# Moving the start addresses of the activation rooms of a routed expert layer: h to 96 and x to 192 modulo 256 bytes

## The chip, the cores and the metric

The kernel runs on one core of one Trainium2 chip. The metric is the device time of one execution in microseconds (us). Lower is better.

## What is computed

The reference is an attention over pooled keys and values, followed by a layer in which each token goes to one of eight experts, if a linear score lets it be computed at all:

```python
# attention: batch 8, 8 heads, 576 positions, head size 64; keys and values pooled by 8 (72 of them)
k_p = k.reshape(B, H, Sp, pool, D).mean(axis=3)
v_p = v.reshape(B, H, Sp, pool, D).mean(axis=3)
scores = scale * np.matmul(q, k_p.transpose(0, 1, 3, 2))
attn = softmax(scores)
x = np.matmul(attn, v_p)              # 4608 tokens of 512
# experts: w1 is 8 x 512 x 1024, w2 is 8 x 1024 x 512
do_compute = x @ w_skip > 0
e_idx = np.argmax(x @ w_gate, axis=1)
h = np.maximum(x[mask] @ w1[e], 0.0)
out = x + gate_w * (h @ w2[e])        # tokens with do_compute; the others keep x
```

## The kernel before

All data are float32. The kernel has two stages.

**Attention** runs over 36 tiles of 128 tokens. Per tile TensorE computes scores (L321), transposes the exponentials (L346, L350) and multiplies with the pooled values (L364, L366), in plain float32. Results are stored to the output by SyncE's queue (`out<-x`), and a routing step sorts the tokens to their experts.

**The experts** run in units of up to three tiles (384 tokens) of one expert. A product in this stage is made of three TensorE products of numbers split in a high and a low part (float32r): high x high, high x low and low x high. The order of work is fixed: a loop over units on each engine, coupled by semaphores. In one unit TensorE does this:

- the **first layer** (`first`, L1136 to L1138): for each of 8 slices f of h and each of 4 slices k of x, three matmuls. The stationary operand is a 128x128 piece of `w1hi` or `w1lo`, the moving operand a slice of `xhi` or `xlo` of as many columns as the unit has tokens, 256, 288, 320 or 384. These are 96 matmuls in a row.
- the **second layer** (`second`, L1151, L1152, L1154): for each tile of 128 tokens and each of 8 slices k of h, two or three matmuls. The stationary operand is a 128x128 piece of `hhi` or `hlo`, the moving operand 512 columns of `w2hi` or `w2lo`.

ScalarE writes `hhi` from the first layer's result (L1192), VectorE writes `hlo` (L1249). ScalarE and VectorE also make `xhi` and `xlo` of the next unit (L1201, L1270) and split the next expert's weights (L1183, L1216). GpSimd gathers tokens into `ring` (L1049) and scatters results (L1054). The first piece of the expert work (L515 to L517, L530 to L532, two tiles of the first expert) is woven into the end of the attention stage and uses the same four rooms and the same weights.

**Where tiles lie.** Tiles of the pool `cp` lie one behind the other along a partition. Four of them are the rooms that the change moves: `xhi`, `xlo` (6144 bytes each in the expert stage) and `hlo`, `hhi` (12288 bytes each). While the attention runs, the same rooms hold inputs: `xhi` and `xlo` are two of the three buffers of q, `hlo` and `hhi` the two buffers of v. The function `early` (L144) makes a room for its first use, and puts an unused tile of `gaps[name]` bytes ahead of it; `late` (L139) makes the room for the experts at the same place. The rooms stand in the order xhi, hlo, xlo, hhi; behind them stand the tiles of the attention's pools.

With the numbers of before, `xhi` and `xlo` begin at 160 modulo 256 bytes, `hlo` and `hhi` at 128. The weights `w1hi`, `w2hi`, `w1lo`, `w2lo` stand ahead of all this and begin at 128 modulo 256. Slices of these tiles are whole multiples of 256 bytes apart (x: 1536 per k, w1: 4096 per k and 512 per f, h: 1536 per k and 512 per tile, w2: 2048 per k), so each operand of the experts' matmuls begins where its tile begins, modulo 256.

Of the kernel before, what the change touches and what calls it, by code (L numbers as in the profile page):

```python
# [110 lines left out]
def emit(tc, q, k, vm, vr, wg, w1, w2, cf, out):  # L111
    nc = tc.nc
    with ExitStack() as top:
        cp = top.enter_context(tc.tile_pool(name="const", bufs=1))
        dp = top.enter_context(tc.tile_pool(name="dram", bufs=1, space=DRAM))
        whi = cp.tile([128, 4, F], F32R, name="w1hi"), cp.tile([128, 8, D], F32R, name="w2hi")
        wlo = cp.tile([128, 4, F], F32R, name="w1lo"), cp.tile([128, 8, D], F32R, name="w2lo")
        table = dp.tile([NE * NTOK + 128, RT], F32, name="table")
        cfs = cp.tile([128, cf.shape[1]], F32, name="cfs")
        wgs = cp.tile([128, 108], F32, name="wgs")  # L120
        c = dict(ident=cfs[:, 0:128], epos=cfs[:, 384:392], first=cfs[:, 392:400], unit=cfs[:, 436:437], place=cfs[:, 443:444], third=cfs[:, 444:445], wgs=wgs,
                 pair=cfs[:, 445 + UNITS:453 + UNITS].rearrange("p (g h) -> p g h", h=2), next=cfs[:, 445:445 + UNITS], left=cfs[0:4 * KL, 439:443])
        c["lower"] = cp.tile([128, 128], BF16, name="upper")
        c["ones"] = cp.tile([128, 128], BF16, name="ones")
        pay = cp.tile([128, NT, RT], F32, name="pay")
        offs = cp.tile([128, NE], F32, name="offs")
        slot = cp.tile([128, SLOTS], I32, name="slot")
        gate = cp.tile([128, SLOTS], F32, name="gate")
        nti = cp.tile([128, 2 * UNITS + 1], I32, name="nti")
        near = dict(ids=cp.tile([128, 2, 2], F32, name="nids"), slot=cp.tile([128, 2], I32, name="nslot"),  # L130
                    first=cp.tile([128, NE], F32, name="nfirst"), jt=cp.tile([128, NE], F32, name="njt"),
                    place=cp.tile([128, 1], F32, name="nplace"))

        stage = cp.tile([128, NST, F], F32, name="stage")
        b = dict(stage=stage)

        gaps = dict(xhi=160, hlo=224, xlo=32, hhi=224)

        def late(name):  # L139

            s, dt = {"x": ([128, 4, 384], F32R), "h": ([128, 8, 384], F32R), "r": ([128, 6, RW], F32)}[name[0]]
            b[name] = cp.tile(s, dt, name=name)

        def early(name, *s):  # L144
            if gaps.get(name):
                cp.tile([128, gaps[name] // 4], F32, name=f"gap{name}")
                gaps[name] = 0
            return cp.tile(list(s), F32, name=name)

        def load_constants():  # L150
            nc.sync.dma_start(cfs[:, 128:], cf[:, 128:])
            nc.sync.dma_start(wgs, wg)

        def spread_constants():
            nc.gpsimd.memset(near["jt"], float(JT))
            nc.gpsimd.memset(nti, 0)
            nc.gpsimd.tensor_copy(c["lower"], cfs[:, 128:256])
            nc.gpsimd.tensor_copy(c["ones"], cfs[:, 256:384])
            nc.gpsimd.memset(pay, 0.0)
            nc.gpsimd.tensor_copy(pay[:, :, 0], cfs[:, 400:436])  # L160
            nc.gpsimd.tensor_copy(offs, c["first"])
            nc.gpsimd.tensor_copy(near["first"], c["first"])

        with tc.manual_schedule(engines={mybir.EngineType.PE, mybir.EngineType.Activation, mybir.EngineType.DVE, mybir.EngineType.Pool}):
            held = attention(tc, nc, q, k, vm, vr, cf, w1, w2, whi, wlo, out, c, pay, offs, table, load_constants, spread_constants, near, b, late, early,
                      dict(slot=slot, gate=gate, nti=nti))
        with tc.tile_pool(name="moeps", bufs=1, space=PSUM) as pp:
            experts(tc, nc, out, w1, w2, whi, wlo, slot, gate, nti, held, near, b, c["ident"], pp)
# [1170 lines left out]
```

## Time and profile before

| | |
|---|---|
| median of 3 runs | 544.38 us (543.05 to 544.89) |
| the profiled execution | 544.18 us |
| its span, from first to last instruction | 542.4 us |
| TensorE (PE) busy | 509.2 us, 94% of the span |
| VectorE, ScalarE, GpSimd busy | 54%, 45%, 40% |
| mean granted TensorE clock | 0.975 |

A busy TensorE in this profile is one that has some matmul in flight: matmuls overlap, so the duration of one is longer than the distance to the next. How fast a stream of matmuls runs is read from the start times in the timeline. The 1.8 us between the time and the span lie ahead of the first and behind the last instruction.

### The profile page before, as it was taken

How to read it: one execution, taken by the hardware profiler on the slowest of the kernel's cores; microseconds unless marked ns; L12 is line 12 of the kernel's file. 1: busy time of each engine (PE TensorE's matmuls, PEld its weight loads, DVE VectorE, ACT ScalarE, POOL GpSimd, SP SyncE). 2: the span in 40 equal slices, each digit the busy share in tenths (PEclk: the TensorE clock that was granted, in tenths of full speed). 3: DMA queues.
4: the chain of work that ended last, by engine and by line, in shares of the span. 5: the costliest groups of instructions: out<-in, count | busy, mean ns of one | idle time of the engine just before them, and what ended most of it. 6: DMA issues, size and time to landing. Idle time of an engine off the chain costs nothing. (4 is left out here: it accounts for less than half of the span.)

```text
span 542.4 us, 10998 instructions
## 1 busy us (share of the span) xinstructions
PE 509.2 (94%) x3350; PEld 460.7 (85%) x3351; DVE 295.2 (54%) x698; ACT 244.2 (45%) x671; POOL 215.6 (40%) x294
## 2 busy tenths in 40 slices
PE   6899999999799888999999999999999999999994
PEld 3789899888688677888989899998989898989893
DVE  4476878877477621344624553232355656665563
ACT  5488889898551011141514142211334435544441
POOL 4725565899966333112321232332321132314042
PEclk8699999999799999999999999999999999999998
DMA  8999979975662111116421551111145647463200
GB/s 293 364 344 338 350 253 368 311 231 195 220 202 70 30 36 51 41 47 209 153 74 39 187 182 63 39 63 51 57 174 162 213 148 271 161 213 104 95 30 7
DMA packets 35799, 87.30 MB, mean 161 GB/s; under 512 B 7529, under 2 KB 9961, under 8 KB 33968
## 3 DMA queue, kind: packets, MB, share of 16 engines
q1 hardware_dynamic: 27648, 72.80, 38.8%
q0 software_dynamic: 8112, 14.03, 8.0%
q8 instruction: 18, 0.29, 0.2%
q14 instruction: 21, 0.17, 0.1%
HBM read 74.04 MB, written 21.52 MB: 176 GB/s over the span
## 5 line engine op out<-in xcount | busy, mean ns | idle before, releaser
L1136 PE MATMUL psl<-xhi,w1hi 128*128 128x256 f32 (+3 forms) x416 | 122.2, 294 | 4.2 <-PEq L965 3.2
L1137 PE MATMUL psl<-xlo,w1hi 128*128 128x256 f32 (+3 forms) x416 | 121.5, 292 | 0.0
L1138 PE MATMUL psl<-xhi,w1lo 128*128 128x256 f32 (+3 forms) x416 | 121.5, 292 | 0.0
L1192 ACT ACTIVATE hhi<-psl 128x256 fp32r<-128x256 f32 (+4 forms) x104 | 41.9, 403 | 152.7 <-ACTq L965 151.7
L1054 POOL DMA_INDIRECT out<-ring,slot x39 | 39.5, 1012 | 176.4 <-POOLq L965 158.9
L1151 PE MATMUL psf<-w2hi,hhi 128*128 128x512 f32 x240 | 94.9, 395 | 2.8 <-PEq L965 2.8
L1152 PE MATMUL psf<-w2lo,hhi 128*128 128x512 f32 x240 | 93.7, 390 | 0.0
L1249 DVE SCALAR_TENSOR_TENSOR hlo<-psl,hhi 128x256 fp32r<-128x256 f32 (+2 forms) x104 | 43.8, 423 | 79.8 <-DVEq L965 79.3
L1136 PEld LDWEIGHTS psl<-xhi,w1hi 128*128 128x128 f32 x416 | 78.3, 188 | 6.1 <-issue 5.5
L1137 PEld LDWEIGHTS psl<-xlo,w1hi 128*128 128x128 f32 x416 | 78.3, 188 | 0.4
L1138 PEld LDWEIGHTS psl<-xhi,w1lo 128*128 128x128 f32 x416 | 78.3, 188 | 0.0
L1154 PE MATMUL psf<-w2hi,hlo 128*128 128x512 f32 x200 | 78.1, 391 | 0.0
L335 ACT ACTIVATE e<-sc,nm 128x72 f32<-128x72 f32 x288 | 64.6, 342 | 0.5 <-DVE nm L328 0.3
L1238 DVE SCALAR_TENSOR_TENSOR ring<-psf,ring 128x512 f32 x25 | 18.7, 750 | 75.5 <-DVEq L965 75.5
L1151 PEld LDWEIGHTS psf<-w2hi,hhi 128*128 128x128 f32 x240 | 45.1, 188 | 11.8 <-issue 3.2
L1152 PEld LDWEIGHTS psf<-w2lo,hhi 128*128 128x128 f32 x240 | 45.1, 188 | 8.6
L1049 POOL DMA_INDIRECT ring<-out,slot x39 | 43.8, 1123 | 16.1 <-issue 12.9
L364 PE MATMUL o<-blocks,pT 128*128 128x148 f32 (+1 forms) x304 | 49.1, 298 | 1.0 <-DVE x L388 0.6
L1201 ACT ACTIVATE xhi<-psd 128x512 fp32r<-128x512 f32 x36 | 18.9, 599 | 68.4 <-ACTq L965 68.4
L328 DVE TENSOR_REDUCE nm<-sc 128x4 f32<-128x288 f32 x72 | 32.4, 453 | 24.8 <-PE sc L321 22.7
L1154 PEld LDWEIGHTS psf<-w2hi,hlo 128*128 128x128 f32 x200 | 37.6, 188 | 8.0
L364 PEld LDWEIGHTS o<-blocks,pT 128*128 128x128 f32 (+1 forms) x304 | 40.9, 183 | 2.9 <-issue 0.8
(220 smaller groups left out, 871.2 us busy)
## 6 DMA issues: line engine op xcount, KB each, us to landing
stage<-in_w SPq DMA_DIRECT2D x64, 512.0 KB, 4.4
out<-x SPq DMA_DIRECT2D x36, 256.0 KB, 4.9
stage<-in_k SPq DMA_DIRECT2D x6, 1152.0 KB, 9.4
hlo<-in_vm SPq DMA_DIRECT2D x4, 1024.0 KB, 8.2
hhi<-in_vm SPq DMA_DIRECT2D x4, 1024.0 KB, 8.6
xlo<-in_q SPq DMA_DIRECT2D x6, 512.0 KB, 5.6
qt<-in_q SPq DMA_DIRECT2D x6, 512.0 KB, 6.8
xhi<-in_q SPq DMA_DIRECT2D x5, 512.0 KB, 7.0
```

The costliest lines, as they stand in the source:

```text
L335: nc.scalar.activation(e[:, h, :], sc[h // 4][:, h % 4 * SP:(h % 4 + 1) * SP], AF.Exp, bias=nm[:, h:h + 1], scale=-1.0)
L364: nc.tensor.matmul(o_[sl, g * 2 * VA:(g + 1) * 2 * VA], pT[:, 2 * a + g, sl], vbd[b % 3][:, 2 * a + g, :], start=(g == 0), stop=False)
L1049: g.indirect_dma_start(ring[:, s % 6, 0:D], None, out, bass.IndirectOffsetOnAxis(ap=slot[:, s:s + 1], axis=0), bounds_check=NTOK - 1, oob_ ...
L1054: g.indirect_dma_start(out, bass.IndirectOffsetOnAxis(ap=offsets, axis=0), ring[:, s % 6, 0:D], None, bounds_check=NTOK - 1, oob_is_err=Fa ...
L1136: t.matmul(ps, whi[0][:, k, w], xhi[:, k, xs], start=(k == 0), stop=False)
L1137: t.matmul(ps, whi[0][:, k, w], xlo[:, k, xs], start=False, stop=False)
L1138: last = t.matmul(ps, wlo[0][:, k, w], xhi[:, k, xs], start=False, stop=(k == 3))
L1151: t.matmul(ps, hhi[:, k, sl], whi[1][:, k, :], start=(k == 0), stop=False)
L1152: last = t.matmul(ps, hhi[:, k, sl], wlo[1][:, k, :], start=False, stop=(short and k == 7))
L1154: last = t.matmul(ps, hlo[:, k, sl], whi[1][:, k, :], start=False, stop=(k == 7))
L1192: a.activation(hhi[:, f, xs], psL[f % 3][:, xs], AF.Relu).then_inc(sem["act"], 1)
L1249: m = v.scalar_tensor_tensor(to[:, f], psL[f % 3][:, cs], 0.0, hhi[:, f, cs].bitcast(F32), ALU.max, ALU.subtract)
```

## The change

Four numbers change, the bytes of the unused tiles ahead of the four rooms. No instruction is added, removed or moved: on every engine the program has the same instructions in the same order, with other addresses.

```diff
-        gaps = dict(xhi=160, hlo=224, xlo=32, hhi=224)
+        gaps = dict(xhi=192, hlo=160, xlo=96, hhi=160)
```

What follows for the starts of tiles, modulo 256 bytes:

| tiles | before | after |
|---|---|---|
| w1hi, w1lo, w2hi, w2lo | 128 | 128 |
| stage, ring | 160 | 160 |
| xhi, xlo | 160 | 192 |
| hlo, hhi | 128 | 96 |
| qt and kp (third buffer of q, pooled keys) | 128 | 96 |
| vl, vs, e, pT, p4, x (the attention's) | 0 | 224 |
| blocks (pooled keys and values as moving operands) | 192 | 160 |

All tiles behind `hhi` move by 32 bytes, since the four gaps sum to 608 bytes in place of 640.

## Rows read from the trace of the kernel before

**Rows 1.** Busy time by stage: the whole program in three stretches (attention, the passage with the first expert work, the units of experts). Columns: the stretch in us, its length, busy us (and instructions) of each engine, granted TensorE clock, share of the DMA engines, GB/s.

```profile
0.00:182.00 182.00, 165.41 (x1255) 149.60 (x1257) 128.95 (x415) 127.89 (x472) 117.54 (x172) 0.94 0.75 264
182.00:220.00 38.00, 32.19 (x191) 27.52 (x190) 11.24 (x24) 6.34 (x14) 11.41 (x15) 0.96 0.15 42
220.00:542.40 322.40, 311.60 (x1908) 283.59 (x1906) 155.01 (x261) 109.95 (x185) 86.61 (x108) 0.99 0.35 117
```

**Rows 2.** What TensorE waited for between 220 and 500 us: us in total, times, longest.

```profile
PE psf L1151 <- PEq L965: 1.1, 1, 1.1
PE psl L1136 <- issue: 0.9, 1, 0.9
PE psl L1136 <- PEq L965: 0.9, 2, 0.5
```

**Rows 3.** Timeline of TensorE, first and last rows of one first-layer pass with 256 columns: start in us, duration, instruction. From the first row to the last there are 96 matmuls.

```profile
356.71 0.28 PE L1136 MATMUL psl<-xhi,w1hi 128*128 128x256 f32 x1
356.83 0.28 PE L1137 MATMUL psl<-xlo,w1hi 128*128 128x256 f32 x1
...
367.80 0.28 PE L1138 MATMUL psl<-xhi,w1lo 128*128 128x256 f32 x1
367.91 0.39 PE L1151 MATMUL psf<-w2hi,hhi 128*128 128x512 f32 x1
```

**Rows 4.** The same of a second pass with 256 columns, and the busy times of the two passes (columns as in the first group).

```profile
437.36 0.28 PE L1136 MATMUL psl<-xhi,w1hi 128*128 128x256 f32 x1
...
448.56 0.39 PE L1151 MATMUL psf<-w2hi,hhi 128*128 128x512 f32 x1
...
356.71:367.91 11.20, 11.20 (x97) 11.20 (x96) 3.72 (x8) 2.70 (x7) 3.49 (x5) 1.00 0.20 67
437.38:448.58 11.20, 11.20 (x98) 11.20 (x97) 7.04 (x11) 6.29 (x11) 3.54 (x5) 1.00 0.44 144
```

**Rows 5.** Timeline, passes with 288 columns (first row, and the first row behind its 96 matmuls), with 320 columns (second matmul and last of the 96, so 94 distances) and with 384 columns (first row, and the first row behind its 96 matmuls).

```profile
460.80 0.30 PE L1136 MATMUL psl<-xhi,w1hi 128*128 128x288 f32 x1
...
473.61 0.39 PE L1151 MATMUL psf<-w2hi,hhi 128*128 128x512 f32 x1
...
225.48 0.31 PE L1137 MATMUL psl<-xlo,w1hi 128*128 128x320 f32 x1
...
239.27 0.31 PE L1138 MATMUL psl<-xhi,w1lo 128*128 128x320 f32 x1
...
403.17 0.34 PE L1136 MATMUL psl<-xhi,w1hi 128*128 128x384 f32 x1
...
420.13 0.39 PE L1151 MATMUL psf<-w2hi,hhi 128*128 128x512 f32 x1
```

**Rows 6.** Timeline of the second layer, first and last of 18 matmuls in a row with 512 columns (17 distances).

```profile
329.62 0.39 PE L1151 MATMUL psf<-w2hi,hhi 128*128 128x512 f32 x1
329.85 0.39 PE L1152 MATMUL psf<-w2lo,hhi 128*128 128x512 f32 x1
...
333.47 0.39 PE L1154 MATMUL psf<-w2hi,hlo 128*128 128x512 f32 x1
```

**Rows 7.** Timeline of the same kind of matmul where the granted clock is 0.5 (five distances from the first row to the last).

```profile
187.79 0.63 PE L530 MATMUL sc<-w2hi,hhi 128*128 128x512 f32 x1
...
189.92 0.63 PE L532 MATMUL sc<-w2hi,hlo 128*128 128x512 f32 x1
```

**Rows 8.** Timeline of the attention's plain float32 matmuls with pooled values (a row joins four matmuls of 148 columns, or two), with the granted clock at 1.

```profile
121.01 0.67 PE L364 MATMUL o<-blocks,pT 128*128 128x148 f32 x4
121.51 0.42 PE L366 MATMUL o<-vl,p 128*128 128x148 f32 x2
121.77 0.41 PE L321 MATMUL sc<-blocks,qt 128*128 128x144 f32 x2
```

**Rows 9.** Groups by line and shape: how many matmuls of each shape there are (L1137 and L1138 have as many as L1136), the weight loads, and the two engines that follow the first layer. Columns: count, busy us, mean ns, idle before.

```profile
L1136 PE MATMUL psl<-xhi,w1hi 128*128 128x256 f32 x256 | 72.0, 281 | 3.3 <-PEq L965 3.2
L1136 PE MATMUL psl<-xhi,w1hi 128*128 128x320 f32 x96 | 29.9, 311 | 0.9 <-issue 0.9
L1136 PE MATMUL psl<-xhi,w1hi 128*128 128x384 f32 x32 | 10.8, 339 | 0.0
L1136 PE MATMUL psl<-xhi,w1hi 128*128 128x288 f32 x32 | 9.4, 295 | 0.0
L1151 PE MATMUL psf<-w2hi,hhi 128*128 128x512 f32 x240 | 94.9, 395 | 2.8 <-PEq L965 2.8
L1152 PE MATMUL psf<-w2lo,hhi 128*128 128x512 f32 x240 | 93.7, 390 | 0.0
L1154 PE MATMUL psf<-w2hi,hlo 128*128 128x512 f32 x200 | 78.1, 391 | 0.0
L1136 PEld LDWEIGHTS psl<-xhi,w1hi 128*128 128x128 f32 x416 | 78.3, 188 | 6.1 <-issue 5.5
L1151 PEld LDWEIGHTS psf<-w2hi,hhi 128*128 128x128 f32 x240 | 45.1, 188 | 11.8 <-issue 3.2
L1249 DVE SCALAR_TENSOR_TENSOR hlo<-psl,hhi 128x256 fp32r<-128x256 f32 x88 | 37.1, 423 | 70.0 <-DVEq L965 69.6
L1192 ACT ACTIVATE hhi<-psl 128x256 fp32r<-128x256 f32 x56 | 21.6, 385 | 76.3 <-ACTq L965 75.6
```

**Rows 10.** DMA queues (packets, MB, share of the time of 16 engines) and the stores of the attention's results (count, KB each, median us from issue to landing). Queue q1 is SyncE's, q0 GpSimd's, which carries the gathers into `ring` and the scatters out of it.

```profile
q1 hardware_dynamic: 27648, 72.80, 38.8%
q0 software_dynamic: 8112, 14.03, 8.0%
...
out<-x SPq DMA_DIRECT2D x36, 256.0 KB, 4.9
```

## Prediction

> **What bounds the kernel now.** I read the busy times by stage first [rows 1]. From 220 us on, 322 of 542 us, TensorE is busy 311.6 of 322.4 us, VectorE half of that and the DMA engines a third. Between 220 and 500 us TensorE waited 2.9 us in all [rows 2], so there the end moves with the pace of the matmuls themselves. The change touches no order and no count. It can move the time only through operations whose duration depends on where an operand begins.
>
> The pace is the distance between starts. With 256 columns, 96 matmuls take 367.91 - 356.71 = 11.20 us, 116.7 ns each [rows 3]. With 288 columns it is 12.81 / 96 = 133.4 ns, with 320 it is 13.79 / 94 = 146.7 ns, with 384 it is 16.96 / 96 = 176.7 ns [rows 5]. The second layer with 512 columns takes 3.85 / 17 = 226.5 ns [rows 6]. Now what a column costs: at the granted clock 0.5 (1.2 GHz) a matmul of 512 columns takes 2.13 / 5 = 426 ns [rows 7], which is 512 / 1.2, one column per cycle and nothing else. At 2.4 GHz that makes 106.7, 120, 133.3, 160 and 213.3 ns. So at the full clock each matmul has an **excess**: 10.0, 13.4, 13.4, 16.7 ns in the first layer (9.4, 11.1, 10.0, 10.4% of the columns' time) and 13.2 ns in the second (6.2%).
>
> Who makes the excess? Not the other engines: two passes with 256 columns take the same 11.20 us, one beside VectorE busy 3.72 us and DMA at 0.20, one beside 7.04 us and 0.44 [rows 4]. The attention's plain float32 matmuls hardly have it: 0.50 us for four of 148 columns, 125 ns [rows 8], against two cycles per column, 123.3 ns. [...] I take it, as an inference, for a cost of TensorE's own two reading streams, moving operand and next weights (one LDWEIGHTS of 188 ns runs under each matmul [rows 9]), and this is what start addresses could touch.
>
> **The change part by part.** What the excess is worth in all: first layer 768 x 10.0 + 288 x 13.4 + 96 x 13.4 + 96 x 16.7 ns (three times the counts of L1136) = 7.7 + 3.9 + 1.3 + 1.6 = 14.5 us, second layer 680 x 13.2 = 9.0 us [rows 9]. No address can give back more than these 23 us; upward there is no such cap in the rows.
>
> *x from 160 to 192.* The moving operand of the first layer began 32 bytes past a multiple of 64; now it begins on one, as the second layer's (w2 at 128) does now. The trace has float32r streams at these two starts alone, so the price is bounded by the two readings. If the excess belongs to the column and to the start, the first layer comes down from about 10% to the second's 6.2%: 256 columns to 113.3 ns (-3.4), 288 to 127.4 (-6.0), 320 to 141.6 (-5.1), 384 to 169.9 (-6.8), which gives 768 x 3.4 + 96 x 6.0 + 288 x 5.1 + 96 x 6.8 = 2.6 + 0.6 + 1.5 + 0.7 = -5.4 us. If the excess belongs to the instruction (10.0 to 16.7 ns against 13.2), the first layer is no dearer than the second and the gain is 0. The shares by column lie in two clear groups (9.4 to 11.1 against 6.2) and the nanoseconds by instruction do not, but the latter rise only from 10 to 17; I stand between the two and take half, -2.7 us. A loss is possible too: the distance from weights to x grows from 32 to 64 bytes, and if a pass got dearer by the smallest difference between neighbours above, 3.3 ns, it would be 1248 x 3.3 = +4.1 us.
>
> *h from 128 to 96.* Here h is the stationary operand. Its weight load has 226.5 ns of matmul above it, where in the first layer the same load of 188 ns fits a pace of 116.7 ns [rows 3, 6, 9]. What hides it is the 512-column matmul; I take 0. If that cover fails, the second layer pays what the first does (rival 2). ScalarE and VectorE write and read h and x too, but follow with 385 and 423 ns per slice [rows 9], under the 12 x 116.7 = 1400 ns of its matmuls, so a few per cent on them stay hidden.
>
> *What moves along.* The attention's tiles behind `hhi` move by 32 bytes. Its moving pieces of one tile begin 592 bytes apart, so at four different places modulo 256 already, and go in one even run at 125 ns [rows 8]: 0. [...]
>
> Faster matmuls start nothing that collides: TensorE's next waits are those of [rows 2], and 2.7 us over 13 units of about 25 us change no order. **Sum**, on the profiled execution: 544.18 - 2.7 = 541.5 us. It stood 0.2 us under the median of the three runs; the difference is below what counts here. A measurement of this kernel tells some 0.3%, 1.6 us, from no change.
>
> **The rivals.**
>
> *1. Addresses do not matter at this step.* The excess depends on shapes, and all five paces stay: 544.2 us. For it: the excess per instruction is nearly flat, and it stays equal over passes. Against it: two groups by share of columns, with starts as the one evident difference beside the shape. [...]
>
> *2. The second layer gets dearer.* Now h and w2 both begin at 128; after, they stand 32 bytes apart, as x and w1 do now. If it is this distance that makes the first layer's share, the second layer goes from 6.2% to the 10.4% of the 384-column pass: 213.3 x 1.104 = 235.5 ns, +9.0 ns x 680 = +6.1 us, so 550.3 us; with half of it, 547.2. It decides from 2.4 ns per second-layer matmul on (1.6 us). Against it: the weight load has room there. For it: nothing in the trace shows h at another start.
>
> [...]
>
> **How the numbers follow.** Chances: the first layer quicker, by 1.6 to 6 us, 0.40 (its own range 538.5 to 542.6); quicker still 0.03; rival 1, 0.30; rival 2 or a dearer first layer 0.23; rival 3, 0.04. So faster 0.43, same 0.30, slower 0.27. The time is that of the first case, 541.5 us. The range goes from its full price, 544.2 - 5.4 = 538.8, rounded down to 538.5, to just under rival 2's full price, 549.5; outside stay the quicker case and perhaps 0.08 of the slower ones.
>
> **What would show it.** In the changed kernel's timeline: the distance of first-layer matmuls with 256 columns between 113.3 and 116.7 ns (I expect about 115), with 320 between 141.6 and 146.7; the second layer at 226.5 ns; the attention's at 125 ns; ScalarE's 385 and VectorE's 423 ns unchanged; landing of `out<-x` near 4.9 us. Wrong if the first layer keeps 116.7 ns (rival 1), if the second layer's distance passes 229 ns (rival 2), or if the first expert unit starts later than now with the matmuls at their old pace (rival 3).

## The result and the profile after

The change made the kernel slower. The median is 547.23 us (545.8 to 548.5) against 543.39 us of before (540.47 to 544.89), nine runs each; the ratio is 1.0076 with a 95% interval of 1.0057 to 1.0095. The medians differ by 3.8 us, the ratio makes +4.1 us. The forecast was 541.5 us, faster.

The page after differs little from the page before. TensorE is busy for the same share, VectorE and ScalarE did the same work:

```profile
PE 511.0 (94%) x3350; PEld 459.0 (84%) x3351; DVE 295.4 (54%) x698; ACT 244.3 (45%) x671; POOL 216.6 (40%) x294
```

What TensorE waited for between 220 and 500 us is 2.9 us, as in [rows 2]:

```profile
PE psl L1136 <- issue: 1.2, 1, 1.2
PE psf L1151 <- PEq L965: 1.0, 1, 1.0
PE psl L1136 <- PEq L965: 0.7, 2, 0.3
```

So no wait was added. The groups by line show where the time is: the second layer's mean durations rose, the first layer's hardly moved (its L1136 took 122.2 us, 294 ns each, before). Columns: count, busy us, mean ns, idle before.

```profile
L1136 PE MATMUL psl<-xhi,w1hi 128*128 128x256 f32 (+3 forms) x416 | 122.0, 293 | 4.2 <-PEq L965 3.0
...
L1151 PE MATMUL psf<-w2hi,hhi 128*128 128x512 f32 x240 | 95.9, 400 | 2.6 <-PEq L965 2.6
L1152 PE MATMUL psf<-w2lo,hhi 128*128 128x512 f32 x240 | 94.8, 395 | 0.0
L1154 PE MATMUL psf<-w2hi,hlo 128*128 128x512 f32 x200 | 79.0, 395 | 0.0
```

In [rows 9] the three groups of the second layer stand at 395, 390 and 391 ns; each is 4 to 5 ns longer now. Since matmuls overlap, the true price is in the **pace**, the time from one start to the next. The timeline after, one long run of 48 second-layer matmuls (start in us, duration, instruction), and behind it the same run of before:

```profile
420.29 0.40 PE L1151 MATMUL psf<-w2hi,hhi 128*128 128x512 f32 x1
420.52 0.39 PE L1152 MATMUL psf<-w2lo,hhi 128*128 128x512 f32 x1
...
431.26 0.39 PE L1154 MATMUL psf<-w2hi,hlo 128*128 128x512 f32 x1
```

```profile
420.36 0.39 PE L1152 MATMUL psf<-w2lo,hhi 128*128 128x512 f32 x1
...
430.79 0.39 PE L1154 MATMUL psf<-w2hi,hlo 128*128 128x512 f32 x1
```

After: 10.97 us over 47 distances, 233.4 ns. Before (from 420.13, where its first layer ends [rows 5]): 10.66 / 47 = 226.8 ns. The granted clock is 1.00 in both stretches. The first layer after, passes with 256, 288 and 384 columns, first row and the row behind the 96 matmuls (of the last the first row alone), and with 320 columns, second matmul and last of the 96:

```profile
356.47 0.28 PE L1136 MATMUL psl<-xhi,w1hi 128*128 128x256 f32 x1
...
367.78 0.39 PE L1151 MATMUL psf<-w2hi,hhi 128*128 128x512 f32 x1
...
461.77 0.30 PE L1136 MATMUL psl<-xhi,w1hi 128*128 128x288 f32 x1
...
474.41 0.40 PE L1151 MATMUL psf<-w2hi,hhi 128*128 128x512 f32 x1
...
403.65 0.34 PE L1136 MATMUL psl<-xhi,w1hi 128*128 128x384 f32 x1
...
223.96 0.31 PE L1137 MATMUL psl<-xlo,w1hi 128*128 128x320 f32 x1
...
237.74 0.30 PE L1138 MATMUL psl<-xhi,w1lo 128*128 128x320 f32 x1
```

These are 11.31 / 96 = 117.8 ns (116.7 before), 12.64 / 96 = 131.7 ns (133.4) and, up to 420.29, 16.64 / 96 = 173.3 ns (176.7). With 320 columns nothing moved: 13.78 / 94 = 146.6 ns (146.7). Averaged over all matmuls of the trace, pauses left out, the second layer went from 227.6 to 233.2 ns, the first layer's 256-column passes from 116.7 to 117.5.

**The sum by paces:** 680 x 5.6 ns = +3.8 us, 768 x 0.75 ns = +0.6 us, 96 x 1.7 ns = -0.2 us, 96 x 3.3 ns = -0.3 us, together +3.9 us. From the first matmul of the first expert pass to the last of the second layer the two profiled executions took 534.14 - 198.74 = 335.4 and 535.77 - 196.73 = 339.0 us, +3.6:

```profile
196.73 0.37 PE L1136 MATMUL psl<-xhi,w1hi 128*128 128x256 f32 x1 [2.31 <-PEq L965]
...
535.77 0.40 PE L1152 MATMUL psf<-w2lo,hhi 128*128 128x512 f32 x1
```

The spans differ by 1.6 us only, because this execution reached the experts 2.0 us earlier. The attention stage varies that much from one execution to the next: in the traces of the four kernels further below that ran where before took 542.9 us, that matmul starts at 194.6, 195.0, 198.0 and 198.0 us. This is why the paces, and not one span, carry the argument below.

### The profile page after: what moved, and what is told of

Its sections match the earlier page's. It is cut to its first block, busy times and chain, and to the rows that moved or that the text cites. A ratio compares the mean times of both kernels' runs of the same rounds, so it can differ in the third digit from the quotient of the medians.

```text
span 544.0 us, 10998 instructions
## 1 busy us (share of the span) xinstructions
PE 511.0 (94%) x3350; PEld 459.0 (84%) x3351; DVE 295.4 (54%) x698; ACT 244.3 (45%) x671; POOL 216.6 (40%) x294
## 5 line engine op out<-in xcount | busy, mean ns | idle before, releaser
L1136 PE MATMUL psl<-xhi,w1hi 128*128 128x256 f32 (+3 forms) x416 | 122.0, 293 | 4.2 <-PEq L965 3.0
L1138 PE MATMUL psl<-xhi,w1lo 128*128 128x256 f32 (+3 forms) x416 | 121.1, 291 | 0.0
L1137 PE MATMUL psl<-xlo,w1hi 128*128 128x256 f32 (+3 forms) x416 | 121.1, 291 | 0.0
L1151 PE MATMUL psf<-w2hi,hhi 128*128 128x512 f32 x240 | 95.9, 400 | 2.6 <-PEq L965 2.6
L1152 PE MATMUL psf<-w2lo,hhi 128*128 128x512 f32 x240 | 94.8, 395 | 0.0
L1136 PEld LDWEIGHTS psl<-xhi,w1hi 128*128 128x128 f32 x416 | 78.0, 188 | 6.2 <-issue 5.6
L1154 PE MATMUL psf<-w2hi,hlo 128*128 128x512 f32 x200 | 79.0, 395 | 0.0
L1137 PEld LDWEIGHTS psl<-xlo,w1hi 128*128 128x128 f32 x416 | 77.9, 187 | 0.5
L1138 PEld LDWEIGHTS psl<-xhi,w1lo 128*128 128x128 f32 x416 | 78.1, 188 | 0.0
L1151 PEld LDWEIGHTS psf<-w2hi,hhi 128*128 128x128 f32 x240 | 45.0, 188 | 12.8 <-issue 3.0
L1152 PEld LDWEIGHTS psf<-w2lo,hhi 128*128 128x128 f32 x240 | 45.1, 188 | 9.8
L1154 PEld LDWEIGHTS psf<-w2hi,hlo 128*128 128x128 f32 x200 | 37.5, 187 | 9.1
```

The costliest lines, as they stand in the source:

```text
L1136: t.matmul(ps, whi[0][:, k, w], xhi[:, k, xs], start=(k == 0), stop=False)
L1137: t.matmul(ps, whi[0][:, k, w], xlo[:, k, xs], start=False, stop=False)
L1138: last = t.matmul(ps, wlo[0][:, k, w], xhi[:, k, xs], start=False, stop=(k == 3))
L1151: t.matmul(ps, hhi[:, k, sl], whi[1][:, k, :], start=(k == 0), stop=False)
L1152: last = t.matmul(ps, hhi[:, k, sl], wlo[1][:, k, :], start=False, stop=(short and k == 7))
L1154: last = t.matmul(ps, hlo[:, k, sl], whi[1][:, k, :], start=False, stop=(k == 7))
```

## The experiments

The experiments ran on three chips. On two of them before takes 555 and 553.5 us. What is more there lies early: in a run below with the paces of before, the 384-column pass begins at 416.20 us where it began at 403.17 [rows 5], 13.0 us later, and the span is 13.0 us longer too (555.4 against 542.4 us). The paces of matmuls with the same addresses agree (second layer with h at 128: 226.8 and 227.0 ns; with h at 96: 233.4 ns twice). Else times are compared on one chip alone. A pace "with 512" below is that of the 48 second-layer matmuls behind the 384-column pass (47 distances), "with 256" that of a settled pass, one in which TensorE makes no pause, "with 384" that of its one pass.

**h alone.**

```diff
-        gaps = dict(xhi=160, hlo=224, xlo=32, hhi=224)
+        gaps = dict(xhi=160, hlo=192, xlo=64, hhi=192)
```

> h moves to 96, x stays at 160. Theory A (the second layer pays for the distance between the starts of h, its stationary operand, and w2, its moving one): second-layer matmuls at the changed kernel's 233.3 ns, first layer at the paces of before (116.7 ns with 256 columns), time about 680 x 5.6 ns = 3.8 us over before, ratio near 1.007. Theory B (x's move, or what lies behind the rooms, makes the loss): second layer stays at 227 to 228 ns, time as before.

Measured: 557.95 us against 555.13 of before, ratio 1.0062 (1.0030 to 1.0094).

```profile
413.71 0.34 PE L1136 MATMUL psl<-xhi,w1hi 128*128 128x384 f32 x1
...
430.67 0.39 PE L1151 MATMUL psf<-w2hi,hhi 128*128 128x512 f32 x1
...
441.64 0.39 PE L1154 MATMUL psf<-w2hi,hlo 128*128 128x512 f32 x1
```

The first layer is that of before (16.96 / 96 = 176.7 ns), the second that of after (10.97 / 47 = 233.4 ns). This part alone makes the loss: theory A.

**x alone.**

```diff
-        gaps = dict(xhi=160, hlo=224, xlo=32, hhi=224)
+        gaps = dict(xhi=192, hlo=192, xlo=64, hhi=192)
```

> x moves to 192, h stays at 128. Theory A: second layer at 227 to 228 ns as before, first layer at the changed kernel's paces (117.8, 131.7, 146.7 and 173.3 ns with 256, 288, 320 and 384 columns), which is 768 x 1.1 - 96 x 1.7 - 96 x 3.3 ns = +0.4 us, so no difference that can be told. Theory B: most of the 4 us of loss is here.

Measured: 555.18 against 555.13 us, ratio 1.0002 (0.9964 to 1.0040).

```profile
414.73 0.34 PE L1136 MATMUL psl<-xhi,w1hi 128*128 128x384 f32 x1
...
431.37 0.39 PE L1151 MATMUL psf<-w2hi,hhi 128*128 128x512 f32 x1
...
442.04 0.39 PE L1154 MATMUL psf<-w2hi,hlo 128*128 128x512 f32 x1
```

173.3 ns with 384 columns, 227.0 ns in the second layer; 117.8 ns with 256. x's part of the change shows at three of the four shapes and is worth nothing in the sum, since the many matmuls with 256 columns lose what the few with 288 and 384 win.

**Weights, x and h all 32 bytes lower.** Unused tiles of 224 bytes ahead of the weights and 32 behind them, so that what follows keeps its place:

```diff
+        cp.tile([128, 56], F32, name="wgap")
         whi = cp.tile([128, 4, F], F32R, name="w1hi"), cp.tile([128, 8, D], F32R, name="w2hi")
         wlo = cp.tile([128, 4, F], F32R, name="w1lo"), cp.tile([128, 8, D], F32R, name="w2lo")
+        cp.tile([128, 8], F32, name="wback")
...
-        gaps = dict(xhi=160, hlo=224, xlo=32, hhi=224)
+        gaps = dict(xhi=128, hlo=224, xlo=32, hhi=224)
```

> Weights, x and h all begin 32 bytes lower than before (96, 128, 96), so every distance between two operands is that of before while no start is. Theory A1 (only distances count): all paces of before, 116.7 ns with 256 columns and 227 to 228 ns in the second layer, and the time of before. Theory A2 (the place of the start itself counts, as by multiples of 64 bytes: h at 96 is off such a multiple as in the changed kernel): second layer at about 233 ns, time about 4 us over before.

Measured: 555.12 against 555.13 us, ratio 1.0016 (0.9982 to 1.0051). The lines of this kernel stand two lower (L1138 is before's L1136).

```profile
416.20 0.34 PE L1138 MATMUL psl<-xhi,w1hi 128*128 128x384 f32 x1
...
433.16 0.39 PE L1153 MATMUL psf<-w2hi,hhi 128*128 128x512 f32 x1
...
443.82 0.40 PE L1156 MATMUL psf<-w2hi,hlo 128*128 128x512 f32 x1
```

176.7 and 226.8 ns, the paces of before, with h at 96 as in the changed kernel. So none of these starts matters by itself. The tiles behind `hhi` stand where the changed kernel has them, so they do not make its loss either.

**The weights alone 32 bytes lower.** The two unused tiles of the last experiment, with the gaps of before.

> Only the weights begin 32 bytes lower (96); x stays at 160, h at 128. The distance from w1 to x is then the changed kernel's 64 bytes, and h stands 32 bytes above w2 where it stands 32 below in the changed kernel. Theory A1: the first layer runs at the changed kernel's paces (117.8 and 173.3 ns with 256 and 384 columns) though x has not moved; the second layer leaves 227 ns, to an unknown side. Theory A2 (absolute start of h or x): both layers keep the paces of before unless the weights' own start off a multiple of 64 costs.

Measured in one run: 558.59 us. The runs of before on this chip go from 551.8 to 559.0 us, so the paces alone tell something here.

```profile
416.45 0.34 PE L1138 MATMUL psl<-xhi,w1hi 128*128 128x384 f32 x1
...
433.10 0.40 PE L1153 MATMUL psf<-w2hi,hhi 128*128 128x512 f32 x1
...
444.06 0.39 PE L1156 MATMUL psf<-w2hi,hlo 128*128 128x512 f32 x1
```

16.65 / 96 = 173.4 and 10.96 / 47 = 233.2 ns: the first layer runs as in the changed kernel though x did not move, and the second layer is as slow with h 32 bytes above w2 as with 32 below (233.4 ns). With the last experiment this shows what counts: the distance, modulo 256, between the starts of the operand that a matmul streams and of those that it has loaded. That the period is 256 bytes was not tried by itself: the slices of one pass stand whole multiples of 256 apart and run at one pace.

**The other places.** Four kernels with other numbers in `gaps`, then two more.

```diff
-        gaps = dict(xhi=160, hlo=224, xlo=32, hhi=224)
+        gaps = dict(xhi=0, hlo=0, xlo=0, hhi=0)       # x at 0, h at 0
+        gaps = dict(xhi=32, hlo=0, xlo=0, hhi=0)      # x at 32, h at 32
+        gaps = dict(xhi=64, hlo=0, xlo=0, hhi=0)      # x at 64, h at 64
+        gaps = dict(xhi=96, hlo=64, xlo=192, hhi=64)  # x at 96, h at 160
+        gaps = dict(xhi=128, hlo=64, xlo=192, hhi=64) # x at 128, h at 192
+        gaps = dict(xhi=224, hlo=0, xlo=0, hhi=0)     # x at 224, h at 224
```

> x and h at 0, no unused tiles at all: w1 to x is -128 (as +128), w2 to h the same. Theory P64 (the distance counts modulo 64 bytes): second layer as before (227.7 ns, a multiple of 64 apart), first layer as with x at 192 (117.8 ns with 256, 173.3 ns with 384 columns). Theory P256 (it counts modulo 256, each place for itself): other paces than the two seen of at least one layer.

> x and h at 32: x stands 96 below w1 (as 160 above), w2 stands 96 above h. Theory P64: first layer as before (116.7 and 176.7 ns with 256 and 384 columns), second layer at 233 ns. Theory P256: paces of their own.

> x and h at 64: 64 below the weights both. Theory P64: first layer 117.8 and 173.3 ns, second layer 227.7 ns. Theory P256: paces of their own.

> x at 96, 32 below w1; h at 160, 32 above w2, which is the distance of the run in which only the weights moved. So the second layer is at 233.1 ns by every theory of distances. First layer: Theory P64 gives 116.7 and 176.7 ns as at +32, Theory P256 a pace of its own.

> x at 128, level with w1; h at 192, 64 above w2. A place of its own for each distance modulo 256: no pace is forecast from the others, but if the second layer at 64 below (229.1 ns) tells of 64 above, it lies under 231 ns. If level were best for both layers, the first layer would fall under 114.3 ns with 256 columns.

> x at 224, 96 above w1; h at 224, 96 above w2. Theory of distances modulo 256: paces of their own; the second layer above 229 ns, since only level (227.7) and 64 below (229.1) were under it so far.

One run each: 544.8, 546.5, 543.7 and 548.0 us beside 542.9 of one run of before, and 557.9 and 558.5 us on a chip where before takes 553.5. By their paces (ns; distance is x - w1 for the first layer and w2 - h for the second):

```
first layer   x at    128    160    192    224      0     32     64     96
              distance  0    +32    +64    +96   +128    -96    -64    -32
   256 columns        119.9  116.7  117.8  119.9  118.7* 118.7  113.6* 118.3
   384 columns        173.4  176.7  173.3  176.6  175.9  176.6  174.7* 173.4
second layer  h at    128     96     64     32      0    224    192    160
              distance  0    +32    +64    +96   +128    -96    -64    -32
   512 columns        226.8  233.4  228.9  233.4  232.3  234.5  233.4  233.2
* not the only pace at this place: x at 64, see the last experiment; x at 0, one pass of four at 120.0
```

The lowest and the highest of the second layer besides level, h at 64 and h at 224 (first and last row of the 48):

```profile
419.63 0.39 PE L1151 MATMUL psf<-w2hi,hhi 128*128 128x512 f32 x1
...
430.39 0.39 PE L1154 MATMUL psf<-w2hi,hlo 128*128 128x512 f32 x1
```

```profile
432.51 0.40 PE L1151 MATMUL psf<-w2hi,hhi 128*128 128x512 f32 x1
...
443.53 0.40 PE L1154 MATMUL psf<-w2hi,hlo 128*128 128x512 f32 x1
```

10.76 / 47 = 228.9 and 11.02 / 47 = 234.5 ns. Theory P64 fell: 64 above and 64 below are not alike (228.9 and 233.4), nor is 128 like level. The guess that +64 tells of -64, under 231 ns, was a miss. h at 128, as before had it, is the best of the eight places, and six of the other seven cost 5.5 to 7.7 ns, the change's among them; there was no neighbour to gain from.

**hlo alone at 96.**

```diff
-        gaps = dict(xhi=160, hlo=224, xlo=32, hhi=224)
+        gaps = dict(xhi=160, hlo=192, xlo=64, hhi=224)
```

> Only hlo goes to 96; hhi stays at 128, x at 160. The weight load of hlo runs under the matmul of L1152, that of hhi under L1151 and L1154. Theory R (a running matmul's read is held up by the next matmul's weight load): the distance from L1152 to L1154 is near 233 ns, those from L1151 and L1154 stay near 227. Theory S (a matmul is slow by the start of its own stationary operand): L1154 is near 233, the other two near 227. Theory T (no single matmul pays, the stream settles on one pace): all three move alike, to some 229 ns.

Measured in one run: 555.42 us beside 553.50 of before.

```profile
430.41 0.39 PE L1151 MATMUL psf<-w2hi,hhi 128*128 128x512 f32 x1
...
440.85 0.39 PE L1151 MATMUL psf<-w2hi,hhi 128*128 128x512 f32 x1
441.08 0.40 PE L1152 MATMUL psf<-w2lo,hhi 128*128 128x512 f32 x1
441.31 0.39 PE L1154 MATMUL psf<-w2hi,hlo 128*128 128x512 f32 x1
```

10.90 / 47 = 231.9 ns, over three quarters of the loss with one stationary operand in three moved. Over the whole trace the distances behind L1151, L1152 and L1154 are 230.1, 231.6 and 232.6 ns (227.6 to 227.7 before). So all three pay, not alike but none alone: closest to theory T. How one tile's start acts on the matmuls with the other is not to be seen from this, and stays open.

**The best place of each layer together,** x at 64 and h at 128.

```diff
-        gaps = dict(xhi=160, hlo=224, xlo=32, hhi=224)
+        gaps = dict(xhi=64, hlo=64, xlo=192, hhi=64)
```

> The best place seen for each layer: x at 64 as in the run with both at 64, h at 128 as before. If the layers' paces are independent: first layer 114.3 ns with 256 and 174.7 with 384 columns, second layer 227.7 ns, so 768 x 2.4 + 96 x 2.0 ns = 2.0 us under before, ratio about 0.996. If they aren't, the first layer's gain does not show.

Measured: 552.89 against 553.50 us, ratio 0.9988 (0.9970 to 1.0006): no difference that can be told. A 256-column pass of the kernel with x and h at 64, then the same pass of this one, first row and the row behind the 96:

```profile
356.85 0.28 PE L1136 MATMUL psl<-xhi,w1hi 128*128 128x256 f32 x1
...
367.76 0.39 PE L1151 MATMUL psf<-w2hi,hhi 128*128 128x512 f32 x1
```

```profile
367.31 0.28 PE L1136 MATMUL psl<-xhi,w1hi 128*128 128x256 f32 x1
...
378.62 0.39 PE L1151 MATMUL psf<-w2hi,hhi 128*128 128x512 f32 x1
```

10.91 / 96 = 113.6 ns against 11.31 / 96 = 117.8 ns, with x and w1 at the same places in both. So the layers' paces are not independent here, and the sum of two best places was a miss. Over all 256-column matmuls, pauses left out, the kernel with both at 64 runs at 114.3 ns, this one at 116.6 and before at 116.7, and the 384-column pass is at 176.7 again: next to nothing of the first layer's gain came. The second layer kept its 227 ns. In this kernel the four passes without a pause run at 117.8 ns, while three that TensorE interrupts in the middle go on at 113.3 ns behind the pause.

## Why the prediction was wrong

**What bounds the kernel** held. The waits stayed at 2.9 us and the change of pace went to the end almost whole: +3.9 us by paces, +3.6 us in the expert stage, +3.8 us by the medians.

**That the excess lies between TensorE's two reading streams** was an inference and is borne out as far as this: the pace follows the distance between the starts of stationary and moving operand, and not either start (second layer: 226.8 ns with weights, x and h moved together, 233.2 ns with the weights moved alone). The distance does not settle it alone, as the last experiment shows (113.6 and 117.8 ns at one distance). No run shows a read that waits for another.

**The excess itself is an estimate.** No run shows TensorE's frequency. What the trace shows is 426 ns for 512 columns at the granted clock 0.5 [rows 7]; halved, that is the 213 ns on which the columns' times at the full clock rest. The two cycles per column of plain float32 are an estimate of the same kind: in the trace of before four such matmuls of 128 columns, at the granted clock 0.50, take 0.85 us, 212.5 ns each, twice the 426 x 128 / 512 = 106.5 ns that float32r would take by [rows 7].

```profile
15.56 1.06 PE L346 MATMUL pt<-cfs,e 128*128 128x128 f32 x4
16.41 0.64 PE L350 MATMUL pr<-cfs,e 128*128 128x128 f32 x2
```

**"h from 128 to 96 ... I take 0" is the step that failed.** I took the weight load as hidden since 188 ns of it lie under 226.5 ns of matmul. It does lie under the matmul as an instruction, and yet the start of what it loads sets the matmul's pace: +5.6 ns x 680 = +3.8 us, nearly all of the loss, and h alone shows it. That the load's reads hold up the matmul's is a guess of mine; no run shows it.

**"x from 160 to 192 ... take half, -2.7 us" failed too.** The reading by columns, that a start on a multiple of 64 gives the second layer's 6.2%, was wrong. With 256 columns the pace rose by 1.1 ns in most passes where I expected up to -3.4; with 288 it fell by 1.7 of 6.0, with 384 by 3.3 of 6.8, with 320 by nothing. x alone is worth +0.1 us by these paces and nothing by the measured times. It was no rule of multiples of 64 at all: with x at 128, level with the weights, the first layer's 256-column passes are at their slowest, 11.51 / 96 = 119.9 ns.

```profile
367.77 0.28 PE L1136 MATMUL psl<-xhi,w1hi 128*128 128x256 f32 x1
...
379.28 0.40 PE L1151 MATMUL psf<-w2hi,hhi 128*128 128x512 f32 x1
```

**Rival 1** fell: the same second-layer matmuls take 226.8 ns with h at 128 and 234.5 ns with h at 224, by addresses alone.

**Rival 2** had place and sign right, and a size of 9.0 ns per matmul, borrowed from the 384-column pass; 5.6 were measured. Its full 550.3 us came out as 547.2. Its sign, a second layer past 229 ns, is what the timeline shows. Its reason held in part: the distance is what counts, but the 32 bytes between x and w1 are not what makes the first layer's share, since level with w1 that layer is slower still (119.9 against 116.7 ns). It shared a chance of 0.23 with a dearer first layer because the weight load seemed to have room; the rows of before could not weigh it, as h stood at one place only. The measured time lies inside the stated range, but only because that range was drawn up to this rival's price; that it does so is no merit of the forecast step.

**Rival 3**, slower stores of the attention, fell; no run shows a price for the place that they begin at. The kernel with weights, x and h all lower stores from the same places as the changed one and cost nothing (ratio 1.0016). In the changed kernel `out<-x` lands after 5.0 us (4.9 before [rows 10]), and the experts of the profiled execution began earlier, not later (196.73 against 198.74 us). The attention's float32 matmuls kept their 125 ns: four from 120.41 to 120.91.

```profile
out<-x SPq DMA_DIRECT2D x36, 256.0 KB, 5.0
...
120.41 0.67 PE L364 MATMUL o<-blocks,pT 128*128 128x148 f32 x4
120.91 0.41 PE L366 MATMUL o<-vl,p 128*128 128x148 f32 x2
```

## What to carry to other kernels

Where TensorE streams float32r at full clock and bounds the time, read its pace from the start times in the timeline, and try the start addresses of stationary and moving operand against each other over all eight steps of 32 bytes: here they span 8 ns of 227 and 6 of 117. That an instruction lies under a longer one did not make it free here (a load of 188 ns under a pace of 227.6 ns, and +5.6 ns with h 32 bytes lower); price it at zero only if a row shows it at another setting. When two rows differ in shape and in address, the difference alone does not tell which of the two made it.

## What the runs showed of the hardware that was not expected

- Many paces come back to a tenth of a nanosecond from pass to pass and from run to run, on different chips: 116.7 or 117.8 ns with 256 columns, 226.7 or 233.3 ns with 512. Two passes beside different loads of VectorE, ScalarE and the DMA engines ran alike, 11.20 us each [rows 4]. The two paces with 512 columns are 13.4 and 20.0 ns over the 213.3 ns that is the estimate for its columns alone (above). Not every place has one such pace: with h at 0 two long runs of the second layer took 232.3 and 233.4 ns.
- A pass can settle at more than one pace with the same operands at the same places: 113.6 or 117.8 ns with x at 64 (above). Even inside one pass it changes. In the changed kernel one 256-column pass of eight begins at 4.12 / 35 = 117.7 ns and, behind a pause of TensorE, goes on at 3.40 / 30 = 113.3 ns; the other seven stay at 117.8 ns. Between the two kernels with x at 64 only h had moved, the second layer's operand; what makes a pass settle at the one pace or the other was not tried.

```profile
254.95 0.28 PE L1136 MATMUL psl<-xhi,w1hi 128*128 128x256 f32 x1
...
259.07 0.28 PE L1138 MATMUL psl<-xhi,w1lo 128*128 128x256 f32 x1
...
262.94 0.28 PE L1136 MATMUL psl<-xhi,w1hi 128*128 128x256 f32 x1
...
266.34 0.28 PE L1136 MATMUL psl<-xhi,w1hi 128*128 128x256 f32 x1
```
